# A gated mix of softmax and linear attention: the listed order made anew with longer landings of SyncE's transfers, and 120 packs on VectorE for 121

## The chip, the cores and the metric

The kernel runs on one core of a Trainium2 chip. The metric is the device time of one execution in microseconds (us); lower is better. A core has five engines that work side by side, each with a queue of its own that it runs strictly in order: TensorE (PE, matrix products), VectorE (DVE), ScalarE (ACT, here the exponential), GpSimd (POOL) and SyncE (SP, here the issue of transfers). They wait for one another by semaphores. A transfer (DMA) that SyncE issues lands some time later, and only then may an instruction that needs its data start.

## What is computed

The input x has 2048 tokens of 512 features, in bf16. Two branches with 32 heads of 16 features each work on it, and a gate per token mixes them:

```
x = A_x
g = _sigmoid((x * gate_w).sum(-1, keepdims=True))
a = _A_ref(x, A_wqkv, A_wo)            # softmax attention over all 2048 tokens, then @ wo
b = _B_ref(x, B_wqkv, B_w_phi, B_wo)   # linear attention
return g * a + (1 - g) * b

# _A_ref, per head:
scores = jnp.einsum("bhqd,bhkd->bhqk", q, k) * (Dh ** -0.5)
p = _softmax(scores, axis=-1)
o = jnp.einsum("bhqk,bhkd->bhqd", p, v)

# _B_ref, per head:
phi_q = jnp.concatenate([_softmax(pq, axis=-1), _softmax(-pq, axis=-1)], axis=-1)   # pq = q @ w_phi
phi_k = ...                                                                          # the same of k
kv = jnp.einsum("bhsf,bhsd->bhfd", phi_k, v);  z = phi_k summed over the tokens
o = (phi_q @ kv) / (phi_q . z + 1e-6)
```

Branch A is nearly all of the work: 32 heads times 2048 x 2048 exponentials.

## The kernel before

**Units and packs.** The queries are cut into 4 chunks of 512 (`QCH`), the keys into 16 tiles of 128. One unit is one head's scores for one tile of keys and one chunk of queries: a PSUM bank of 128 keys x 512 queries. Four heads side by side (in the four row groups of PE) make a pack, so there are 4 x 8 x 16 = 512 packs (`NPACK`). The 16 packs of one group of four heads and one chunk add their products of values into one bank; then the group is normalised (`_norm_a`, `_norm`).

**Two ways to an exponential.** Most packs go to ScalarE: the units run through a ring of five PSUM banks, and one ACTIVATE takes three units, the next two, in turn (`_qk`, `_exp`, line 1020). The other packs go to VectorE, which builds an approximate exponential from bit patterns: per unit one TENSOR_SCALAR turns scores into an integer whose bits are a bf16 number (`_vector_bits`, tile va, line 912), and three additions of constants per pair of packs give three shifted copies whose sum is a better exponential (`_vector_terms`, tile vp, line 928). PE then sums over four terms for such a pack and over one for a pack of ScalarE's (`_values`, line 1086). `AWAY` says which packs go to VectorE: one number for each of the 32 groups, whose five low bits stand for the packs 1, 4, 7, 10 and 13 of the group. `_plan_vector` collects a group's chosen packs in pairs; an odd one out stays alone.

**Side work.** In the cover of the exponentials run the projections of later heads (`_proj_k`, `_proj_v`, `_proj_q`), the gate (`_gate`), and branch B: features of k and their sums (`_b_quad`, `_b_kv`), features of q (`_b_quad`, `_b_phit`), their product with the sums (`_b_num`) and the output product (`_b_out`, `_out`), whose result is added to branch A's in PSUM.

**SyncE's transfers.** SyncE issues: copies of each projected q from qs into qT, which spread heads over the partitions (`_proj_q`, line 677, eight transfers each time); the gate's copies into gh (line 756, sixteen); the copies of normalised outputs from T2 into turned (`_norm`, line 1126, sixteen each time) and their transpose into onTA; the transposes of phi into phiT (`_b_phit`) and of branch B's results nb into WT (`_b_num`), all transposes through `_turn` (line 1341); the loads, and the stores of the output (line 1450).

**What sets the order.** Nothing in the program is ordered at run time. A planner (`Plan.order`) simulates the five queues once, before the program is written, and each engine then runs its list as planned. Each operation has an estimated cost, a due time (`prio`, in packs) and a landing (`lat`): the time after its planned end at which users on another engine may start. The planner takes the operation that can start first, and among those that could start at about that time the one with the smallest due time:

```
r = d.end + (d.lat if d.eng != e or e == "SP" else 0.0 if e == "PE" else self.CHAIN)
...
if o.ready <= t0 + 0.02 + (self.NEAR if pe else 0.0):
    more = self.COST * (o.until - array.SWITCH - base - o.cost) if pe else 0.0
    key = (o.prio + more, seq[id(o)])
```

So an estimate changes no instruction and no wait of the program: a semaphore still holds each user until its data is there. It changes only the places in the lists. `SHIFT` is a table that moves the due time of tagged pieces of work, in packs: p is a pack's product with its values, b the bits, t the terms and x the product with the terms of a pack on VectorE, k, v and q projections, g a group's normalisation, and d, e, a, f, h, n, o, w and y pieces of branch B and of the output. Three PSUM banks outside the ring are shared by all side work.

Of the kernel before, what the change touches and what calls it, by code (L numbers as in the profile page):

```python
# [376 lines left out]
class _Kernel:  # L377
# [10 lines left out]
    TURN = 1.5  # L388
# [278 lines left out]
    def _proj_q(self, qc, cp):  # L667
        n = qc * 4 + cp
        due = 32 * n + self.QDUE
# [7 lines left out]
        parts = [lambda e, r=r: e.dma_start(self.qT[r:r + DH, s0 + r // DH % 2, :], tile[r:r + DH, :])  # L677
                 for r in range(0, P, DH)]
        self.dma("SP", f"q{n}", parts, cost=0.63 * len(parts), reads=[self.b_qs[n % 2]], writes=[self.b_qT[s0]],
                 prio=due, lat=1.6)  # L680
# [44 lines left out]
    def _gate(self):  # L725
# [22 lines left out]
        for r, sign in ((0, -1.0), (1, 1.0)):  # L748
# [5 lines left out]
               prio=self.GATE + 4)  # L754
# [3 lines left out]
        d = self.dma("SP", "gate", parts, cost=0.6 * len(parts), writes=[self.b_g], deps=[a], prio=self.GATE + 5, lat=1.6)  # L758
        for b in self.b_onTA[0] + self.b_onTA[1]:
# [7 lines left out]
           prio=26)  # L767


    AWAY = (15, 5, 27, 9, 19, 31, 28, 28, 26, 27, 23, 27, 22, 30, 31, 22, 15, 15, 23, 7, 31, 23, 23, 7, 27, 31, 11, 27, 15, 31, 23, 31)  # L770

    SHIFT = (
# [723 lines left out]
```

## Time and profile before

| | |
|---|---|
| median of 3 runs | 760.5 us (760.5 to 760.85) |
| the profiled execution | 759.62 us |
| its span, first to last instruction | 757.8 us |
| ScalarE busy | 740.5 us (98%), 646 instructions |
| VectorE busy | 728.9 us (96%), 1130 instructions |
| PE busy (matmuls) | 716.8 us (95%), 7199 instructions |
| PE clock granted | 1.00 throughout |
| SyncE: qT, turned (issue, median to landing) | 0.59 and 0.60 us, 1.8 us |
| transposes: phiT, WT, onTA (median to landing) | 3.3, 2.5, 2.4 us |

"Busy" is the share of the span in which an engine has an instruction under way. A row of a group reads: line, engine, operation, output and input tile with their shapes, count | busy us, mean ns of one | idle time of the engine just before those instructions, and what ended it. In the timeline a row is a run of instructions: start, duration, engine, line, operation, and in brackets the wait before the first of them. "Landing" is counted from the start of a transfer's issue. In the chain, which is followed back from the last instruction, each piece is released by the one before it.

### The profile page before, as it was taken

The page shows a single profiled execution, that of the slowest core. Times are in us where ns is not written, and L with a number is a line of the kernel's source. Part 1 is how long each engine was busy: PE and PEld are TensorE (multiplying, and loading weights), DVE is VectorE, ACT ScalarE, POOL GpSimd, SP SyncE. Part 2 cuts the span into 40 slices and gives each one's busy share as a digit, 9 for nine tenths or more (in the row PEclk, how much of TensorE's full clock was granted, in tenths as well). Part 3 has the DMA queues.
Part 4 walks back from the last instruction along what each step waited for, and adds up shares of the span by engine and source line. Part 5 has one row for each costly group of instructions (what it writes and reads, how often), then busy time and mean ns, then how long its engine had stood idle before and what let it go on. Part 6 is the DMA issues. An engine that isn't in the chain of part 4 may idle for free.

```text
span 757.8 us, 16834 instructions
## 1 busy us (share of the span) xinstructions
PE 716.8 (95%) x7199; PEld 229.7 (30%) x7266; DVE 728.9 (96%) x1130; ACT 740.5 (98%) x646; POOL 7.8 (1%) x17
## 2 busy tenths in 40 slices
PE   8999999999899999999998999999999999999997
PEld 3343333233232322232222322222322322322322
DVE  6999999999999999999999999999999999999997
ACT  5999999999999999999999999999999999999996
POOL 3000000000000000000000000000000000000000
PEclk9999999999999999999999999999999999999999
DMA  9401001000010010100122111410203201131110
GB/s 196 147 6 15 9 1 16 8 3 13 9 15 8 5 18 2 15 8 4 20 24 47 23 16 21 84 22 9 35 17 72 41 8 22 37 63 22 11 26 29
DMA packets 90027, 21.78 MB, mean 29 GB/s; under 512 B 82912, under 2 KB 89440, under 8 KB 89952
## 3 DMA queue, kind: packets, MB, share of 16 engines
q1 hardware_dynamic: 88224, 20.17, 14.2%
q8 instruction: 57, 0.93, 0.5%
q10 hardware_dynamic: 1728, 0.52, 0.3%
q14 instruction: 18, 0.15, 0.1%
HBM read 4.21 MB, written 2.10 MB: 8 GB/s over the span
## 4 chain that ended last, share of the span: by engine, by line
ACT 63%; DVE 17%; PE 17%; DMA 2%; issue 1%; DVEq 0%
ACT ET L1020 60%; DVE va L912 7%; PE ps L972 6%; PE ps L1086 5%; DVE vp L928 4%; ACT bq L1259 3%; PE ps L641 2%; DMA WT<-nb 1%; DVE nb L1371 1%; DVE T L1107 1%; DMA xT<-in_A_x_dram 1%; DVE btree L1248 1%; PE ps L714 1%; PE ps L1389 1%; PE ps L1093 1%
## 5 line engine op out<-in xcount | busy, mean ns | idle before, releaser
L1020 ACT ACTIVATE ET<-ps 128x1536 bf16<-128x1536 f32 x626 | 712.2, 1340 | 8.5 <-PE ps L972 7.3
L972 PE MATMUL ps<-qT,kT 32*128 32x512 bf16 x2048 | 315.1, 384 | 16.2 <-ACT ET L1020 9.6
L912 DVE TENSOR_SCALAR va<-ps 128x512 uint16<-128x512 f32 x484 | 315.2, 684 | 9.6 <-PE ps L972 7.8
L928 DVE TENSOR_SCALAR vp<-va 128x4096 uint16<-128x4096 uint16 (+1 forms) x204 | 221.9, 1099 | 2.0 <-PE ps L1086 1.5
L972 PEld LDWEIGHTS ps<-qT,kT 32*128 32x128 bf16 x2048 | 81.3, 91 | 266.5 <-ACT ET L1020 156.0
L1086 PE MATMUL ps<-ET,V 128*32 128x512 bf16 x1564 | 150.2, 386 | 0.3 <-DVE va L912 0.3
L1086 PE MATMUL ps<-vp,vc 128*32 128x512 bf16 x968 | 86.1, 384 | 0.5 <-DVE vp L928 0.4
L1086 PEld LDWEIGHTS ps<-ET,V 128*32 128x32 bf16 x1564 | 39.6, 94 | 66.3 <-issue 53.7
L641 PE MATMUL ps<-WB,xT 128*128 128x512 bf16 x171 | 50.2, 383 | 4.2 <-issue 2.2
L1093 PE MATMUL ps<-kT,zero 128*32 128x512 bf16 x604 | 53.0, 385 | 0.0
L1086 PE MATMUL ps<-va,V 128*32 128x512 bf16 x484 | 47.4, 385 | 0.0
L1086 PE MATMUL ps<-vp,V 128*32 128x512 bf16 x484 | 47.0, 383 | 0.0
L641 PE MATMUL ps<-xT,WA 128*128 128x512 bf16 (+1 forms) x107 | 31.3, 374 | 4.8 <-issue 2.4
L1086 PEld LDWEIGHTS ps<-vp,vc 128*32 128x32 bf16 x968 | 22.3, 95 | 34.7 <-issue 20.7
L1259 ACT ACTIVATE bq<-bq 128x2048 bf16<-128x2048 bf16 x16 | 31.6, 1992 | 0.0
L1107 DVE STREAM_TRANSPOSE T<-ps 128x512 f32<-128x512 f32 x32 | 22.7, 708 | 1.6 <-PE ps L1086 1.5
L1230 DVE CAST bq<-ps 128x512 bf16<-128x512 f32 x32 | 21.7, 684 | 0.3 <-PE ps L641 0.2
L714 PE MATMUL ps<-WA,xT 128*128 128x128 bf16 x256 | 20.4, 220 | 0.7 <-DVE V L720 0.3
L1093 PEld LDWEIGHTS ps<-kT,zero 128*32 128x32 bf16 x604 | 13.7, 94 | 21.7 <-issue 19.6
L641 PEld LDWEIGHTS ps<-WB,xT 128*128 128x128 bf16 x192 | 12.6, 97 | 24.4 <-issue 12.9
L1257 DVE TENSOR_TENSOR bq<-bq,btree 128x2048 bf16<-128x2048 bf16 x16 | 19.5, 1219 | 0.0
L1389 PE MATMUL ps<-WoB,WT 128*128 128x512 bf16 x58 | 16.8, 382 | 2.6 <-DMA WT<-nb 1.1
(83 smaller groups left out, 338.0 us busy)
## 6 DMA issues: line engine op xcount, KB each, us to landing
turned<-T SPq DMA_DIRECT2D x240, 8.0 KB, 1.8
qT<-qs SPq DMA_DIRECT2D x120, 16.0 KB, 1.8
WB<-in_B_wqkv_dram SPq DMA_DIRECT2D x1, 1536.0 KB, 7.6
out_dram<-WB SPq DMA_DIRECT2D x12, 128.0 KB, 1.9
WA<-in_A_wqkv_dram SPq DMA_DIRECT2D x3, 384.0 KB, 5.9
WoA<-in_A_wo_dram SPq DMA_DIRECT2D x1, 512.0 KB, 7.7
WoB<-in_B_wo_dram SPq DMA_DIRECT2D x1, 512.0 KB, 8.6
WA<-in_A_wqkv_dram ACTq DMA_DIRECT2D x3, 128.0 KB, 4.2
```

Source lines behind the costliest of these rows:

```text
L641: ins = e.matmul(self._bank(job)[:, 0:n], lhs(c), rhs(c), start=(c == 0), stop=(c == 3))
L714: ins = e.matmul(self._bank(job)[:, P * tt:P * tt + P], self.xT[:, c, QCH * j + TOK * tt:QCH * j + TOK * tt + TOK], self.WA[:, 2, c, P * c ...
L912: parts.append(op("DVE", lambda e, j=j, job=job: e.tensor_scalar(self.va[:, pair, side, j, :], self._bank(job), SCALE * LOG2E * 128.0, (12 ...
L928: self.plan.op("DVE", lambda e, k=k, shift=shift: e.tensor_scalar(flat(self.vp[:, k]), flat(self.va[:, pair]), float(shift), None, op0=ALU ...
L972: return e.matmul(out, self.kT[32 * i:32 * i + 32, cp, kt * TOK:(kt + 1) * TOK], self.qT[32 * i:32 * i + 32, s, :], start=True, stop=True, ...
L1020: o = plan.op("ACT", lambda e: e.activation(self.ET[:, a % NS:a % NS + n, :], self.ps[:, self._ring(a):self._ring(a) + n, :], ACT.Exp, sca ...
L1086: ins = e.matmul(self._bank(ot)[32 * i:32 * i + 32, :], V[:, v0:v0 + 32], tile(), start=(kt == 0), stop=(kt == self.NT - 1), tile_position ...
L1093: ins = e.matmul(self._bank(ot)[32 * i:32 * i + 32, :], self.zero[:], self.kT[:, 0, 0:QCH], start=False, stop=False, tile_position=(0, 32 ...
L1107: op("DVE", lambda e: e.transpose(T1[:, side].rearrange("p b s -> p (b s)"), src()), 0.635, deps=last, writes=[b_T1[side]], name="n_t1", p ...
L1230: [lambda e, b, k=k: e.tensor_copy(bq[:, k].rearrange("p (g s v) -> p g s v", g=8, s=2)[:, :, 0, :], b.rearrange("p (g v) -> p g v", g=8))],
L1259: op("ACT", lambda e, side=side: e.activation(sides[side], sides[side], ACT.Exp, scale=1.0 - 2 * side), self.c_act(2048) + 0.04, reads=[bu ...
L1389: return e.matmul(self._bank(job), self.onTB[:, pr, tt * TOK:tt * TOK + TOK], self.WoB[:, pr, :], start=(pr == 0), stop=False)
```

## The change

Five estimates of landings after transfers on SyncE are longer, the table of packs on VectorE is another, with 120 packs where there were 121, and the table of shifts is another: of 708 entries 45 keep key and value, 161 keys are gone and 155 keys are new. No line that builds an instruction is changed.

```diff
-    TURN = 1.5
+    TURN = 2.2
...
         self.dma("SP", f"q{n}", parts, cost=0.63 * len(parts), reads=[self.b_qs[n % 2]], writes=[self.b_qT[s0]],
-                 prio=due, lat=1.6)
+                 prio=due, lat=2.6)
...
-        d = self.dma("SP", "gate", parts, cost=0.6 * len(parts), writes=[self.b_g], deps=[a], prio=self.GATE + 5, lat=1.6)
+        d = self.dma("SP", "gate", parts, cost=0.6 * len(parts), writes=[self.b_g], deps=[a], prio=self.GATE + 5, lat=4.0)
...
-    AWAY = (15, 5, 27, 9, 19, 31, 28, 28, 26, 27, 23, 27, 22, 30, 31, 22, 15, 15, 23, 7, 31, 23, 23, 7, 27, 31, 11, 27, 15, 31, 23, 31)
+    AWAY = (15, 5, 27, 26, 20, 27, 14, 28, 30, 13, 23, 31, 14, 14, 30, 31, 29, 14, 23, 7, 31, 27, 23, 23, 30, 31, 11, 27, 11, 31, 23, 31)
...
     SHIFT = (
-        ("p12", 2), ("k5", -3), ("k4", -9.5), ("v1", -6.5), ("p30", -8), ("p13", -1), ("p22", 1), ("q1", 3), ("w0",
-        -14), ("p18", -8.5), ("b1", -7.5), ("v2", -5), ("x1", -4), ("v4", 6), ("p21", -3), ("p2", 0.5), ("k1", -5),
...
+        ("k5", -3), ("k4", -10), ("v1", -6.5), ("p30", -4.5), ("p13", 7), ("p22", 8.5), ("q1", 3.5), ("w0", -10),
+        ("p18", -11.5), ("b1", -7.5), ("v2", -5), ("x1", -5), ("v4", 6), ("p21", -3), ("p2", 0.5), ("k1", -6),
...
             self.dma("SP", f"on{due:.0f}", parts, cost=0.68 * len(parts), reads=[b_T2], writes=[self.b_turned], prio=due,
-                     lat=1.6)
+                     lat=2.2)
...
         self.b_phiT.writers.append(self._turn(
             f"ph{t}", self.phiT[:, :, t % 4 * TOK:t % 4 * TOK + TOK], self.bq[:, k, :], self.b_bq[0:2],
-            self.phit_war, due, lat=2.2))
+            self.phit_war, due, lat=3.2))
```

`TURN` is the landing of every transpose for which `_turn` is given none: those of nb into WT and of turned into onTA. The transposes that load x have landings of their own, which stay.

185 rows, old and new, of the table SHIFT are left out of this document.

## The prediction

> **What bounds the kernel now.** I read the page's busy shares first, then the groups by shape for ScalarE, the waits of ScalarE and VectorE, the chain of waits, and last the timeline around the two longest gaps of ScalarE inside the run.
>
> From the page, the busy shares:
>
> ```profile
> span 757.8 us, 16834 instructions
> PE 716.8 (95%) x7199; PEld 229.7 (30%) x7266; DVE 728.9 (96%) x1130; ACT 740.5 (98%) x646; POOL 7.8 (1%) x17
> ```
>
> ScalarE (ACT) is idle for 17.3 us in all, VectorE (DVE) for 28.9. Both are nearly full, and ScalarE is the fuller. The groups of ScalarE by shape (busy us, mean ns | idle us before them), and then what ScalarE waited for (us in total, times, longest):
>
> ```profile
> L1020 ACT ACTIVATE ET<-ps 128x1536 bf16<-128x1536 f32 x313 | 485.6, 1551 | 7.7 <-PE ps L972 6.6
> L1020 ACT ACTIVATE ET<-ps 128x1024 bf16<-128x1024 f32 x312 | 352.3, 1129 | 0.7 <-PE ps L972 0.7
> L1020 ACT ACTIVATE ET<-ps 128x512 bf16<-128x512 f32 x1 | 0.8, 758 | 0.0
> ```
>
> ```profile
> ACT ET L1020 <- PE ps L972: 7.3, 6, 5.1
> ACT xT L1445 <- PE ps L1435: 3.7, 1, 3.7
> ```
>
> The exponentials take three score units, then two, in turn. Of the 7.3 us that they wait, 5.1 is the start (the first one begins at 8.71 us). That leaves five waits, 2.2 us, in all the time from 8.71 to the end of the last exponential at 750.20. Start and tail (750.20 to 757.8, 7.6 us, one head's normalisation, the last output product and its store) are set by loads and by a chain that the change does not shorten.
>
> The pace of ScalarE when nothing disturbs it, and what led to the two longest gaps, is in the chain of waits:
>
> ```profile
> 99.64 76.89 ACT ET L1020 x68
> 429.50 3.52 DMA WT<-nb
> 547.72 3.95 DMA WT<-nb
> ```
>
> 68 exponentials are 34 pairs of a three and a two: 76.89/34 = 2.26 us a pair. The transposes of nb into WT on SyncE landed 3.52 and 3.95 us after their issue, and the timeline shows ScalarE stopped soon after each:
>
> ```profile
> 433.12 0.48 DVE L1371 SCALAR_TENSOR_TENSOR nb<-ps,ghb,rb 128x256 bf16<-128x256 f32 x1 [0.73 <-DMA WT<-nb]
> 434.33 1.45 ACT L1020 ACTIVATE ET<-ps 128x1536 bf16<-128x1536 f32 x1 [0.51 <-PE ps L972]
> 551.81 1.02 PE L1389 MATMUL ps<-WoB,WT 128*128 128x512 bf16 x4 [1.09 <-DMA WT<-nb]
> 554.49 1.02 ACT L1020 ACTIVATE ET<-ps 128x1024 bf16<-128x1024 f32 x1 [0.72 <-PE ps L972]
> ```
>
> **All that an order can win.** 312 pairs at 2.26 us are 705.6; the last three adds 1.34 to the start of the single one, which takes 0.76 to its end; the 16 long exponentials of branch B cost 1.80 each (two take 3.60 in the chain), 28.8; the gate's one about 0.1. Together 736.6. From 8.71 to 750.20 are 741.5 us, so 4.9 us are lost inside: the 2.2 of the five waits, some 0.2 at each of them because an exponential no longer overlaps the next one, and small delays. Whatever the order, only these 4.9 us can come back.
>
> **The change, part by part.**
>
> One pack fewer on VectorE. The bits of the table of packs sum to 121 before and 120 after, so ScalarE has 4 x 392 = 1568 units for 1564: 314 threes and 313 twos, and no single. Where the single one began, now a two begins and a three ends the row. The two takes 2.26 - 1.34 = 0.92 to the next start, the three 1.55 to its end, against 0.76 before: 0.92 + 1.55 - 0.76 = 1.7 us more. This lies on the path whole: ScalarE's row between start and tail has only the 4.9 us of holes, and the tail begins at its end. VectorE loses four TENSOR_SCALAR of the bits (0.60 us apart in the chain, 2.4 us); there are 68 pairs of packs before and after, but 16 instead of 15 hold a single pack, so three term additions shrink from 1.17 to 0.69 us, 1.4 us. So 3.8 us less on VectorE, which is busy 702.5 of the 720 us from 20 to 740; it is not the row that ends the run, so I count it at nothing. The PE trades twelve tile matmuls of the three terms for four, two rows of four at 0.22 us, 0.4 us less, hidden beside ScalarE.
>
> The longer landings, place by place. They change no transfer, only when the planner expects a transfer's users to be ready, and so where it lists them.
> - Copies of q (1.6 to 2.6 us after the last issue; eight issues of 0.59 us, landing 1.8 median, 3.5 at most): the first score that needs a q stands 22 packs behind its projection by the due times, about 30 us at 724/512 us a pack, so both landings are hidden. Zero; if that cover were gone, 1.0 us a copy.
> - The gate's copies (1.6 to 4.0): issued from 38.9 to 48.6, landed 1.8 later, and the first transpose into onTA, which must follow them, is issued at 73.8. Zero.
> - Copies into turned (1.6 to 2.2) and their transpose into onTA (1.5 to 2.2): the only waiter seen is SyncE's own queue (10.4 us in 8 waits). Behind such a wait stand the next issues of SyncE: transposes of phi and nb, q, stores. It issues 120 q copies at 0.59, 240 turned at 0.60 and 47 transposes at about 1.25, some 274 us of 757.8, so it has room. Zero, with at most 0.6 us for each transpose queued there.
> - Transposes into phiT (2.2 to 3.2): planned at 1.31 + 2.2 = 3.5 us from issue, measured 3.3 median and 4.9 at most; no matmul that reads phiT shows a wait for a DMA. No gain; listed 1.0 us later its four users are covered by fills and values.
> - Transposes of nb (1.5 to 2.2): planned before at 1.25 + 1.5 = 2.75 us from issue, now at 3.45; measured 2.5 median. The two late ones missed the plan by 0.77 and 1.20 and stopped ScalarE for 0.51 and 0.72. With 0.70 us more room 0.7/0.77 of the one and 0.7/1.20 of the other would go: 0.46 + 0.42 = 0.9 us. Next late there is VectorE's own backlog: beside 553.64 it is in two term additions of 2.36 us.
>
> On the landing the Trainium skill (DMA: Bandwidth & Descriptors, "Anatomy of one DMA") has a rule that speaks against the change: a fixed 2.0 us and the bytes over 436 thousand per us, fitted on GpSimd's path. By it a 128 KB transpose lands in an estimated 2.3 us, the plan before covers every one, nothing comes back, and the sum is +1.7. The trace differs (2.4 to 3.9), and by its rows the sum of these two parts is 1.7 - 0.9 = +0.8.
>
> The new order. Of 708 shifts 45 keep key and value; the packs on VectorE differ in 15 out and 14 in. Which waits the new order has, the trace cannot show. Lower bound: none but landings, so the other 4.9 - 1.2 = 3.7 us go. Upper bound: the whole loss comes a second time, +4.9. I take the loss as it was, 4.9 in all: the two late landings are chances of this order (the median of the sixteen is 2.5 us), three of the five waits, 0.95 us, had nothing to do with SyncE, and the nearest row for another order over the same engines is this one. So the 0.9 is not credited.
>
> **Sum.** 757.8 + 1.7 = 759.5 us of span. The profiled execution took 759.62 with 1.8 outside its span, so 761.3; the median of the runs shown, 760.5, lies 0.9 above it, so 762.2 us, +0.22%. About 0.2%, 1.5 us, is what a measurement of this kernel can tell from no change, so this stands just on the slower side.
>
> **Rivals.**
> - No change that can be told: the 0.9 us of nb come back and no new wait takes their place: 760.5 + 0.8 = 761.3. For it: both long gaps do follow a landing. Against: a different order meets other late landings.
> - Faster: VectorE's 3.8 us of room pay on ScalarE. PE's weight loads for scores waited 35.7 us in 100 times for a bank that the bits on VectorE free, and those scores stand in PE's queue ahead of ScalarE's. If VectorE is never behind, the loss falls from 4.9 to about 1.3 (the waits not due to late banks or landings): 760.5 + 1.7 - 3.6 = 758.6. It decides where the loss is 1.7 us or less. For it: stretches of 77 and 51 us run without any loss. Against: two thirds of all the holes must go, over half of which are shorter than the page shows.
> - Slower by much more: a transpose of nb is queued on SyncE behind the eight issues of a q (5.00 us at 550.59), or behind a copy that waits for VectorE (up to 28.1 us for one). PE's queue is in order, so the output product and the scores behind it wait; one such case is 5.0 us less some 1.3 of an exponential under way, 3.7: 762.2 + 3.7 = 765.9. For it: one product already stopped PE for 1.09 us here. Against: the planner knows SyncE's queue and its costs (0.63 for 0.59).
> - The change does less than it says: the planner may place most users where they stood. Then only the pack is left, 762.2 again.
>
> **How the numbers follow.** Loss as before, or the change doing little: 0.41. Much slower: 0.12. Together slower 0.53. Same: 0.31. Faster: 0.16. The predicted time is 762.2. The ends are 762.2 - 4.9 = 757.3 and 762.2 + 4.9 = 767.1; leaving out about a tenth on each side I cut to 758.7 (the faster case) and 766.2 (the much slower one, a little over). The slower cases alone reach from 762.1 to 766.2.
>
> **What would show it.** 627 exponentials, 314 of 1536 columns and 313 of 1024, 480 bits, 204 term additions. The first exponential near 8.7 us, 7.6 us from the last one's end to the end. Five or so waits of ScalarE with 2 us in all: right. If they sum to under 0.5 us and ScalarE's row from first to last exponential is below 740 us, the faster rival holds. If SyncE's landings no longer stand ahead of a gap and nothing else does, the second. A single gap of ScalarE over 2 us with a DMA ahead of it shows the much slower one. The prediction would be wrong at its root if the spacing of the exponentials changed from 2.26 us a pair, or if the tail or start moved by over 1 us.

## The result, and the profile after

The changed kernel takes 757.51 us (median of 6 runs, 757.35 to 758.27), the kernel before 760.5 (759.91 to 762.88 beside it). The ratio is 0.9959 with a 95% interval of 0.9945 to 0.9972: 0.4% faster. The prediction was 762.2, 0.2% slower, with a range from 758.7: it missed in sign and in range. Run again later the changed kernel took 757.66, a ratio of 0.9957 (0.9942 to 0.9973).

The page of the changed kernel, its busy shares and the chain by engine:

```profile
span 755.7 us, 17044 instructions
PE 719.6 (95%) x7307; PEld 232.0 (31%) x7368; DVE 723.2 (96%) x1126; ACT 740.9 (98%) x647; POOL 7.8 (1%) x17
...
ACT 93%; PE 5%; DVE 1%; DMA 1%; issue 0%; DVEq 0%
```

In the chain of before ScalarE had 63%, VectorE and PE 17% each; now it is ScalarE almost alone. The groups of ScalarE by shape, and what ScalarE waited for (us in total, times, longest):

```profile
L1019 ACT ACTIVATE ET<-ps 128x1536 bf16<-128x1536 f32 x314 | 500.0, 1592 | 5.6 <-PE ps L971 5.3
L1019 ACT ACTIVATE ET<-ps 128x1024 bf16<-128x1024 f32 x313 | 367.2, 1173 | 0.0
...
ACT ET L1019 <- PE ps L971: 5.3, 2, 5.0
ACT xT L1444 <- PE ps L1434: 4.1, 1, 4.1
```

The counts are those forecast, 314 and 313. Of the five waits of before inside the row (0.28, 0.51, 0.72, 0.22 and 0.45 us) only the first is left, 0.28 at 13.5 us. The chain of waits now has stretches of the exponentials that run from one feature block of branch B to the next without a break:

```profile
235.18 80.45 ACT ET L1019 x71
...
368.91 91.76 ACT ET L1019 x81
...
567.71 84.54 ACT ET L1019 x75
```

**Where the time went.** The first exponential starts at 8.62 us (8.71 before) and the last ends at 747.69 (750.20), so the row took 739.07 us for 741.49, though it holds one pack more. By the prediction's pace (76.89/34 = 2.2615 us a pair) the work is 313 x 2.2615 + 1.55 + 28.8 + 0.1 = 738.3, so the loss inside fell from 4.9 to 0.8 us. The tail grew from 7.6 to 8.05. Together, span against span: 1.7 more work - 4.1 loss + 0.4 tail - 0.1 start = -2.1 us. The other 0.9 us between the medians is that the profiled execution of before (759.62) was one of its better ones: over all batches with it the kernel before ran from 758.9 to 765.7 with medians from 760.5 to 761.2, while the changed one stayed within 757.3 to 758.3. Two executions of the kernel before, of 1164.49 and 3253.5 us, stand outside this and are left out everywhere.

**Who waited for a transfer.** These are all waits for transfers among the engines' waits, first of the kernel before, then of the changed one:

```profile
POOL bq L574 <- DMA wphi<-in_B_w_phi_dram: 12.2, 1, 12.2
PEld ps L641 <- DMA xT<-in_A_x_dram: 1.4, 1, 1.4
PE ps L1389 <- DMA WT<-nb: 1.1, 1, 1.1
PE ps L641 <- DMA xT<-in_A_x_dram: 0.9, 1, 0.9
DVE nb L1371 <- DMA WT<-nb: 0.7, 1, 0.7
PEld ps L691 <- DMA xT<-in_A_x_dram: 0.4, 1, 0.4
```

```profile
POOL bq L574 <- DMA wphi<-in_B_w_phi_dram: 11.8, 1, 11.8
PEld ps L641 <- DMA xT<-in_A_x_dram: 1.1, 1, 1.1
POOL bq L728 <- DMA gw<-in_gate_w_dram: 0.6, 1, 0.6
PEld ps L691 <- DMA xT<-in_A_x_dram: 0.3, 1, 0.3
PE ps L641 <- DMA xT<-in_A_x_dram: 0.2, 1, 0.2
```

Only the loads at the start are left. To see the third case, which the waits put down to another engine, I laid the planner's own list beside the trace: each operation's planned start, shifted by as much as the exponentials around it ran behind plan, tells when its engine stood ready. In the kernel before three landings came after their first user stood ready: nb of token tile 1 by 0.75 us, nb of tile 7 by 1.20, and the transpose of turned into onTA of the last pair of groups but one by 0.64. Right behind them the spacing of the exponentials was 0.79, 1.04 and 0.76 us longer than usual, 2.6 us in sum. The visible idle time there is only 0.51, 0.72 and 0.45, because an exponential that is not held up overlaps the one before it. The third case in the trace of before:

```profile
728.82 1.27 SPq L1341 DMA_TRANSPOSE onTA<-turned  x1
...
731.69 0.38 PE L1389 MATMUL ps<-WoB,WT 128*128 128x512 bf16 x1 [0.86 <-DVE T L1107]
...
732.44 1.45 ACT L1020 ACTIVATE ET<-ps 128x1536 bf16<-128x1536 f32 x1 [0.45 <-PE ps L972]
```

The transpose landed at 731.23, and the instruction on VectorE that the trace names ended at 731.29; the product on PE depends on the transpose and not on that instruction.

In the changed kernel no landing after the loads overtook a user on an engine; the closest came some 0.6 us ahead. Two things did this, and the longer estimates are only one of them. The transposes of nb that stopped the kernel before are not slow in the new order: nb of tile 1 landed 3.2 to 4.0 us after its issue in each of the six profiles with the order of before, and 2.4 in each of the five with the new order, where its user also has 5 us of room. There nb of tile 3 is the slow one (3.5 to 3.7 us, 2.5 before), with 21 us of room. Had every user in the changed kernel stood earlier by what the estimates differ (0.7 us behind a transpose of nb or turned, 1.0 behind one of phi or the copies of a q, 2.4 behind the gate's), only the gate's copies, near the start, and those of three q would have come late there, by 1.4 us and by at most 0.4 us.

### The profile page after: what moved, and what is told of

It is laid out like the page before. It is cut to its first block, busy times and chain, and to the rows that moved or that the text cites. A ratio compares the mean times of both kernels' runs of the same rounds, so it can differ in the third digit from the quotient of the medians.

```text
span 755.7 us, 17044 instructions
## 1 busy us (share of the span) xinstructions
PE 719.6 (95%) x7307; PEld 232.0 (31%) x7368; DVE 723.2 (96%) x1126; ACT 740.9 (98%) x647; POOL 7.8 (1%) x17
## 4 chain that ended last, share of the span: by engine, by line
ACT 93%; PE 5%; DVE 1%; DMA 1%; issue 0%; DVEq 0%
ACT ET L1019 89%; ACT bq L1258 4%; PE ps L971 1%; PE ps L1085 1%; DMA xT<-in_A_x_dram 1%; PE ps L714 1%; PE ps L1388 0%; PE ps L1434 0%; PE ps L641 0%; DVE va L911 0%; PE ps L992 0%; DVE kT L664 0%; DVE qT L697 0%; ACT xT L1444 0%; DVE V L720 0%
## 5 line engine op out<-in xcount | busy, mean ns | idle before, releaser
L911 DVE TENSOR_SCALAR va<-ps 128x512 uint16<-128x512 f32 x480 | 311.5, 680 | 12.0 <-PE ps L971 9.5
L927 DVE TENSOR_SCALAR vp<-va 128x4096 uint16<-128x4096 uint16 (+1 forms) x204 | 219.2, 1086 | 0.9 <-PE ps L1085 0.6
L1092 PE MATMUL ps<-kT,zero 128*32 128x512 bf16 x744 | 63.3, 384 | 0.0
L641 PE MATMUL ps<-xT,WA 128*128 128x512 bf16 (+1 forms) x114 | 33.2, 375 | 2.8 <-issue 1.6
L1092 PEld LDWEIGHTS ps<-kT,zero 128*32 128x32 bf16 x744 | 16.0, 94 | 25.1 <-issue 22.2
L714 PEld LDWEIGHTS ps<-WA,xT 128*128 128x128 bf16 x256 | 15.1, 98 | 10.4 <-issue 6.9
```

What stands on the lines that cost most here:

```text
L641: ins = e.matmul(self._bank(job)[:, 0:n], lhs(c), rhs(c), start=(c == 0), stop=(c == 3))
L714: ins = e.matmul(self._bank(job)[:, P * tt:P * tt + P], self.xT[:, c, QCH * j + TOK * tt:QCH * j + TOK * tt + TOK], self.WA[:, 2, c, P * c ...
L911: parts.append(op("DVE", lambda e, j=j, job=job: e.tensor_scalar(self.va[:, pair, side, j, :], self._bank(job), SCALE * LOG2E * 128.0, (12 ...
L927: self.plan.op("DVE", lambda e, k=k, shift=shift: e.tensor_scalar(flat(self.vp[:, k]), flat(self.va[:, pair]), float(shift), None, op0=ALU ...
L1092: ins = e.matmul(self._bank(ot)[32 * i:32 * i + 32, :], self.zero[:], self.kT[:, 0, 0:QCH], start=False, stop=False, tile_position=(0, 32 ...
```

## Experiments

Three theories stand against each other. Late landings: the gain is that no landing overtakes its user. VectorE's room: the gain is the pack fewer. Denser tables: the new shifts would be better whatever the landings are. Where a run removes a wait, it does so by letting the transfer read x and write unused room, so the products of branch B and of some heads come out of stale data there; the amount of work, the lists and the sizes stay.

### Three late transposes that nobody waits for

```diff
+    ASIDE = ('dma_nb1', 'dma_nb7', 'dma_at481')
...
+        for o in p.queues["SP"]:
+            if o.name in self.ASIDE:
+                out, src = free.pop().rearrange("p (t q) -> p t q", t=4), self.xT[:, 3, D:2 * D]
+                o.fn = lambda e, out=out, src=src: e.dma_start_transpose(out, src)
+                aside.append(o)
+        for q in p.queues.values():
+            for o in q:
+                o.deps = [d for d in o.deps if d not in aside]
```

> The kernel before, its lists unchanged. Three transposes on SyncE (nb of token tile 1 and 7 into WT, turned into onTA of the last pair of groups but one) keep their places and sizes but read x and write unused room, and nobody waits for them; the products that used them read what stood there. Theory of late landings: in the trace of before these three landed 0.75, 1.20 and 0.64 us after the time at which their first user stood ready in its list, 2.6 us in sum, and ScalarE lost 0.79, 1.04 and 0.76 us right behind them; so about 2.6 us faster, span near 755.2, and no wait of ScalarE of over 0.3 us between its first and last exponential. Theory of VectorE's room: nothing on VectorE has changed, so within 0.4 us of before. Theory that the new tables are simply denser: also within 0.4 us.

The names are those of nb of tile 1 and 7 and of the transpose into onTA; `free` holds unused room.

Measured: 758.59 us (757.28 to 759.28), ratio 0.9955 (0.9938 to 0.9971), by the medians 2.6 us below before, the size forecast by late landings. The three holes were gone from the profile, but it had a new one: the span is 757.4 and not 755.2, and ScalarE waited 1.07 us at 462.34. PE had stood for a q:

```profile
458.70 0.59 SPq L694 DMA_DIRECT2D qT<-qs  x1
...
460.82 0.39 PE L989 MATMUL ps<-qT,kT 32*128 32x512 bf16 x1 [1.07 <-DMA qT<-qs]
...
461.25 0.69 DVE L929 TENSOR_SCALAR va<-ps 128x512 uint16<-128x512 f32 x1 [1.34 <-PE ps L989]
...
462.34 1.45 ACT L1037 ACTIVATE ET<-ps 128x1536 bf16<-128x1536 f32 x1 [1.07 <-PE ps L989]
```

The last copy of the eleventh q was issued at 458.70, 2.1 us behind the list's plan, and landed 2.1 us later. Its first user is a score for VectorE's bits, which the list has only 0.37 us behind the planned landing. So the kernel before has a fourth weak place, which its own profiled execution did not show: there this q landed 0.35 us in time. Places that give way in one execution and not in the next would make its runs scatter; the run without all four waits, below, bears this out.

### A control: three other transposes

> The same edit on three other transposes of the same kinds (nb of token tile 2 and 3, turned into onTA one pair of groups earlier), which landed before their users stood ready. Every theory: no change, within 0.4 us of before, and the waits of ScalarE at about 433.8, 553.8 and 732 us are still there.

Measured: 759.8 (759.02 to 761.78), ratio 0.9984 (0.9970 to 0.9998). That is 1.2 us below before by the ratio, outside the 0.4 us expected. So the control is not clean: about a third of the gain of the run above (3.4 us by its ratio) may come with the edit itself, or with landings of these three transposes that are late in some executions; this was not tried further. One of the three, nb of tile 2, came only 0.13 us ahead of its user in the profile of before. By the medians the run above is still 1.2 us below the control. The holes behind nb 1 and turned into onTA were there (0.74 and 1.20 us in the spacing) and one behind the q (0.78). The one behind nb 7 was not: in this run that transpose landed in time. So the expectation of three fixed places was too simple; the places are weak, and which of them give way changes from run to run.

### Less work on VectorE

```diff
+        m = n - 100 * (self.pairs > 12)
...
-                flat(self.vp[:, k]), flat(self.va[:, pair]), float(shift), None, op0=ALU.add),
+                flat(self.vp[:, k])[:, 0:m], flat(self.va[:, pair])[:, 0:m], float(shift), None, op0=ALU.add),
```

The run leaves out the last 100 columns of the term additions.

> The kernel before, its lists unchanged. From the 13th pair of packs on, the term additions on VectorE leave out their last 100 columns: 168 instructions shorter by some 23 ns, 3.9 us less work on VectorE, as much as one pack fewer takes off. Theory of VectorE's room: 2 to 4 us faster, ScalarE's loss down to about 1.5. Theory of late landings: under 0.6 us faster, because the three large holes of ScalarE wait for transfers and not for VectorE. Theory of denser tables: under 0.6 us.

Measured: 762.25 (759.15 to 764.10), ratio 1.0003 (0.9985 to 1.0021): no gain, and a gain of 2 us lies outside the interval. VectorE had its room (term additions of 217.0 us for 221.9, busy 726.4 for 728.9), and ScalarE's loss in the profiled execution was larger, 6.9 us: all four weak places gave way, by 1.27, 1.06, 1.19 and 1.30 us. Room on VectorE does not help against a landing.

### More work on VectorE in the changed kernel, first dose

> The changed kernel, its lists unchanged, with 68 very short writes added on VectorE, one ahead of every third term addition: at some 0.06 us each about 4 us more on VectorE, as much as one pack more. Theory of VectorE's room: 2 to 4 us slower than the changed kernel, so near before's time (759.5 to 761). Theory of late landings: up to 1 us slower than the changed kernel (757.5 to 758.5), and no wait of ScalarE over 0.5 us.

Measured: 757.88 (757.37 to 758.36), ratio 0.9951 (0.9934 to 0.9969). This tells nothing on VectorE's room, because the dose failed: the 68 short writes began and ended while the instruction ahead of them still ran, and busy VectorE rose by 0.6 us only.

### The same with a true dose

```diff
+                if k == 0:
+                    e.tensor_scalar(self.more[:, self.mores:self.mores + 1], self.iden[:, 0:1], 1.0, None, op0=ALU.add)
+                    self.mores += 1
```

> The run with short writes on VectorE again with a true dose: there the 68 writes began and ended within the instruction ahead of them and cost VectorE nothing (busy 723.8 for 723.2). Now each of the 68 reads a column and adds a constant, at an estimated 0.06 to 0.1 us each 4 to 7 us more on VectorE, one pack's worth or more. Theory of VectorE's room: 2 to 5 us slower than the changed kernel (759.5 to 762.5). Theory of late landings: within 1 us of it (757 to 758.5), no hole of ScalarE over 0.5 us between 14 us and its last exponential.

Measured: 758.26 (757.87 to 758.92), ratio 0.9962 (0.9950 to 0.9974), about 0.7 us above the changed kernel, which ran in another batch. The 68 instructions now push the next one back by 63 ns each (median), 4.3 us in sum, a pack's worth. ScalarE still has no wait but the start and one of 0.3 us. With the run of less work, VectorE's room is refuted in both directions, as the cause of a gain of this size.

### Four waits away, and then a pack

The q of the first experiment was taken out in the same way.

> As the run without the three waits, and the copies of the eleventh q into qT go the same way (they read x, write unused room, nobody waits): in that run they landed 1.59 us after the first score that needs them stood ready, at 459 us, and ScalarE lost 1.39 us there. Theory of late landings: span near 755.2, no wait of ScalarE over 0.3 us between 14 us and its last exponential, 3 to 4.5 us faster than before by the medians, and runs that scatter by no more than the changed kernel's (0.9 us). Rival, that a hole shut in one place opens in another: within 0.5 us of the run without the three waits, with a new hole elsewhere.

Measured: 757.90 (757.45 to 758.24), ratio 0.9957 (0.9942 to 0.9972), by the medians 2.9 us below before, just under the 3 to 4.5 forecast. The span of the profiled run, 756.1, is 0.9 above the forecast, 0.3 of it a later start (first exponential at 9.03 us) and 0.25 the tail. All holes of the four places are gone, with no new one, and the scatter is 0.8 us in 5 runs, for 3.5 in 17 of before:

```profile
L1040 ACT ACTIVATE ET<-ps 128x1536 bf16<-128x1536 f32 x313 | 487.0, 1556 | 7.0 <-PE ps L992 5.9
L1040 ACT ACTIVATE ET<-ps 128x1024 bf16<-128x1024 f32 x312 | 354.0, 1135 | 0.0
```

So the old list with 121 packs, cured of its late landings alone, gains 2.9 us, and the whole change gains 3.0. The row lost 2.6 us instead of 4.9. That the two gains agree is partly chance: the change also pays for a pack and finds a denser list, and these two nearly cancel, as the next run and the account of the prediction show.

```diff
-    AWAY = (15, 5, 27, ..., 27, 15, 31, 23, 31)
+    AWAY = (15, 5, 27, ..., 27, 7, 31, 23, 31)
```

> The same with one pack fewer on VectorE (number 28 of the table of packs, its fourth bit: the lists differ only from about 650 us on). By the price of a pack on ScalarE's row: 1.2 to 1.8 us slower than the run without the four waits, span 756.4 to 757.0. Theory of VectorE's room: the 3.9 us less on VectorE shut as much on ScalarE, so within 0.5 us of it.

Measured: 759.12 (758.69 to 759.57), ratio 0.9978 (0.9968 to 0.9987), 1.2 us above the run without the four waits. The row grew by 1.2 us (739.21 to 740.38): 1.7 of work, 0.5 less loss. A pack fewer on VectorE is a cost, somewhat below the 1.7 us worked out. Whether the 0.5 us comes from VectorE's room or from the other order behind 650 us was not tried.

### Transposes made late in the changed kernel

```diff
+    LATER = ('dma_nb2', 'dma_nb7', 'dma_at481')
...
+            if o.name in self.LATER:
+                extra = [lambda e, out=room.pop(): e.dma_start_transpose(out, self.xT[:, 3, D:2 * D])
+                         for _ in range(2)]
+                o.fn = extra + [o.fn]
```

> The changed kernel, its lists unchanged, with three transposes made late: ahead of nb of token tile 2 and 7 and of turned into onTA of the last pair of groups but one, SyncE issues two more transposes of the same size (of x, into unused room), 2.5 us of issue, and the users wait for all. They had landed 1.23, 1.09 and 0.91 us before their users stood ready, so they come 1.3, 1.4 and 1.6 us too late. Theory of late landings: ScalarE loses that about one for one behind each, 3 to 4.5 us slower than the changed kernel (760.5 to 762), with holes near 460, 556 and 731 us. Theory of VectorE's room or of denser tables: within 0.6 us of the changed kernel.

Measured: 764.62 (763.33 to 766.74), ratio 1.0050 (1.0031 to 1.0068), 7 us above the changed kernel: the mechanism as forecast, the size above the range. What ScalarE waited for, and the place of the largest wait:

```profile
ACT ET L1032 <- PE ps L984: 11.8, 6, 5.0
...
736.29 1.44 PE L1401 MATMUL ps<-WoB,WT 128*128 128x512 bf16 x3 [2.31 <-DMA onTA<-turned]
...
738.32 1.45 ACT L1032 ACTIVATE ET<-ps 128x1536 bf16<-128x1536 f32 x1 [3.00 <-PE ps L984]
...
742.16 6.88 ACT L1032 ACTIVATE ET<-ps 128x1536 bf16<-128x1536 f32 x6 [1.31 <-PE ps L984]
```

Behind the two nb the spacing of the exponentials was 1.23 and 1.53 us longer for some 1.4 and 1.55 us of lateness: one for one. Behind the transpose into onTA it was 4.6 us for about 2.1. There PE stood for 2.31 us, and from about 735 to 742 us the clock granted to it, 1.00 until then, was halved. Stretches of the trace show it: from and to, length, busy time of PE, PEld, DVE, ACT and POOL with counts, the granted clock, the DMA share and GB/s.

```profile
728.00:735.00 7.00, 5.53 (x56) 1.79 (x54) 6.74 (x11) 7.00 (x7) 0.00 (x0) 1.00 0.40 79
735.00:742.00 7.00, 5.71 (x19) 1.17 (x19) 2.84 (x4) 2.79 (x3) 0.00 (x0) 0.51 0.07 16
742.00:750.00 8.00, 7.76 (x95) 2.33 (x91) 7.38 (x13) 7.84 (x7) 0.00 (x0) 1.00 0.01 2
```

At the halved clock the three matmuls of the output product took 1.44 us, where three of the same shape take 0.82 at 1.00 (at 732.46 us in the first run above), the scores behind them were slower too, and ScalarE ran dry a second time. The forecast of one for one has no such term. How the 4.6 us divide between the stop and the clock was not tried apart. What lowers the clock is not shown either: it fell within this stop, while the stops of 1.46 and 1.73 us behind the two nb came with no lower clock.

The scatter is back too (3.4 us), and a lower clock goes with the slow end of it. Of the 26 runs of the kernel before beside the first experiments, the eight slowest, from 762.17 us up, were all granted 0.998 or less on average (0.993 in the slowest), and of the other 18 all but one 0.999 or more.

### Each part of the change alone

> The kernel before with the five longer landings alone: its table of packs (121) and its shifts stay. If longer landings by themselves are the cure, the late landings go and nothing else: near 757.9, as in the run without the four waits. If the shifts only fit the landings that they were made for, the planner's list itself comes out loose: it has ScalarE stand for 6.2, 2.3, 2.1 and 1.1 us at four places, and the last exponential 16 us later than in the list before, with side work left over behind it, so 30 to 40 us slower than before (790 to 800). No landing comes after its user stood ready in either case.

> The changed kernel with the five landings of before: its tables (120 packs, the new shifts) stay. If the new tables are a better list whatever the landings are, near 757.5 to 760. If they only fit their landings, the list has ScalarE stand for 10.7, 9.5, 5.5, 5.0, 3.1 and 2.2 us at six places, and the run takes 800 to 810 us.

Measured, one run each: 805.0 us for the landings alone and 816.47 for the tables alone, somewhat beyond the expected 790 to 800 and 800 to 810. The planner's times are those at the full clock, and the granted one was 0.974 and 0.988 on average (0.50 from 775 to 792 us in the first, in the work left over at the end). In the first that work is what shows most, in the second ScalarE's holes:

```profile
ACT xT L1445 <- PE ps L1435: 27.7, 1, 27.7
ACT ET L1020 <- PE ps L972: 21.9, 19, 6.1
```

```profile
ACT ET L1019 <- PE ps L971: 30.2, 15, 9.4
ACT bq L1258 <- DVE bq L1256: 19.4, 3, 10.8
```

None of the parts is good alone: the shifts were made for one set of landings, and under another the list falls apart. So the new tables are not better whatever the landings are, and these two runs do not sum to the change. They do bear on the landings: laid beside its list as above, the first has no landing that overtook its user (the closest came 0.5 us ahead, as expected), and in the second nb of tile 1 landed 4.3 us after its issue and 1.6 us late, with the granted clock at 0.57 from 454 to 462 us behind it. That fits longer estimates as what keeps landings ahead of their users, but the two lists differ in everything else as well.

### The longer landings with 121 packs

The groups 28 to 30 of the table of packs hold one pack more, and 195 shifts in the later part differ, chosen by the planner's own end.

> The five longer landings with 121 packs: the changed kernel with one pack more on VectorE (the groups 28 to 30 of the table of packs changed), and shifts made anew for the last part of the list, with the planner's end as the only measure. In that list the last exponential comes 0.8 us earlier than in the changed kernel's and the end 0.8 us later. If the gain of the change lies in the landings and not in the pack: no landing overtakes a user, runs scatter by about 1 us, and the time is 0.3 to 1.3 us above the changed kernel run beside it, well below before (757.8 to 759). If the 120 packs carry the gain: near before, 760 or more.

> The changed kernel once more, beside the run with 121 packs on the same chip. Every theory: 757.3 to 758.3.

Measured: 758.83 (758.21 to 760.06), ratio 0.9971 (0.9960 to 0.9983) with 121 packs; 757.66 (757.33 to 758.27) for the changed kernel beside it. With 121 packs 1.9 us of the changed kernel's 3.0 us are there, so the gain is not the pack's. Two things were not as expected: the runs scatter by 1.9 us and not 1, with the two slowest at a granted clock of 0.997, and one landing overtook its user, a transpose of phi by 0.3 us, with no hole behind it; the transpose into onTA that is the third weak place of before came only 0.04 us ahead. The row of ScalarE is 0.6 us shorter than the changed kernel's (738.46 for 739.06) and the tail 1.5 longer (9.56 for 8.05), as in the list. No version here beats the changed kernel.

## Why the prediction was wrong

- That ScalarE bounds the kernel, and that only its loss inside the row can come back, held: the loss went from 4.9 to 0.8 us, and start and tail moved by 0.1 and 0.4.
- The pack was priced at 1.7 us and counted on the path. The row holds 1.7 us more work in the changed kernel, and the run with the waits away lost 1.2 us by it. VectorE's 3.8 us were counted at nothing, which both doses nearly bear out (no gain for less work, 0.7 us for 4.3 more).
- **The step that failed is the one on the new order: "I take the loss as it was, 4.9 in all", with the 0.9 us of the nb transposes not credited.** The late landings were worth 2.3 us of the profiled row (741.49 to 739.21 without them) and 2.9 of the median. They were not "chances of this order": the list before places users 0.1 to 0.4 us behind planned landings that are too short, and in each of the four profiles that keep all or some of these waits at least one of the four places gave way, in the profiles of the changed kernel none. The median of the sixteen transposes, 2.5 us, hid that nb of tile 1 is slow in every profile of this order. The argument by the nearest row, that another order over the same engines loses as much, is what should have been doubted, since the change lengthens just the estimates that this order breaks on.
- Three terms beneath it were mis-sized. The holes were read from visible idle time (1.23 us for the two nb) where the spacing lost 1.83. The copies of q were set to zero because the first score stands 22 packs behind: that holds for ScalarE's scores, but scores for VectorE's bits are listed far ahead, and the eleventh q had 0.37 us of room, which failed in three of the four profiles here that wait for it. And the transpose into onTA was set to zero because only SyncE's queue was seen to wait, while the trace put PE's wait at 731.69 down to VectorE; it was the third hole, 0.76 us, and one of the three waits said to have nothing to do with SyncE. It landed a normal 2.42 us after its issue. It was late because SyncE issued it 1.1 us behind the plan; in the changed kernel it is issued 1.2 us behind plan and still lands 1.1 us ahead of its user.
- The remaining gain lies in the list itself. Between the run with 120 packs and four waits away and the changed kernel the row shrank from 740.38 to 739.07, 1.3 us. So the row goes from 741.49 by 2.3 us less for the landings, 1.2 more for the pack and 1.3 less for the list to 739.07. The planner's own list for before has 2.98 us of gaps between exponentials, for the changed kernel 1.55, 1.4 us less. That the new shifts are a better find there is read from the lists and rows and was not tried apart. The planner itself has the changed kernel no faster: in its list the last exponential ends 0.3 us later than before and the end comes 0.8 us later, so by its own times there was nothing to gain, and what the runs gained is what the kernel before loses beyond its plan.
- The median of before was taken as the profiled time plus a constant 0.9. It is no constant: it vanished with the late landings (757.54 profiled for a median of 757.51 in the changed kernel, 757.90 for 757.90 with the four waits away).
- Of the rivals, the faster one had its sign and nearly its place (758.6 for 757.5) by a wrong mechanism; the one with the nb transposes had the right mechanism and credited a third of it. The much slower one, a transpose stuck on SyncE, occurred only where it was made.
- The Trainium skill's rule (DMA: Bandwidth & Descriptors, "Anatomy of one DMA — SWDGE (gpsimd) path"), a fixed 2.0 us and the bytes over 436 thousand per us, was fitted on GpSimd's path and puts these transposes at an estimated 2.3 us. No run here is on that path, and on SyncE it is no bound: transposes of 128 KB from nb landed between 2.4 and 4.5 us after their issue in these runs, and it is the late ones that cost. Why one lands at 2.4 and another at 4 us stays open. It is not mere chance, since nb of tile 1 is slow in every profile of one order and of tile 3 in every one of the other.

## What to carry to other kernels

Where the order of work is fixed ahead of time, an estimate of a transfer's landing should cover the late landings and late issues, not the median: a user listed too early stops an in-order engine and all behind it, and the stop can cost more than it lasts when the clock falls behind it. Before judging a list, count for each transfer how much room its first user has and compare it with the spread of landings of that same transfer over several runs; in this case the kernel whose runs scattered was the one that waited for transfers. Here tables tuned against one set of estimates were worth nothing under another, so such a change is to be judged as a whole.

## What was not expected of the hardware

- An instruction's duration is not its price. In the changed kernel the exponentials' mean durations are 1592 and 1173 ns against 1551 and 1129 before, and the median spacing from one to the next is the same (1.33 and 0.90 us). The unbroken row is not the reason, since with the true dose the row has no more breaks and the means are 1558 and 1138 ns; what is stays open.
- A write of one constant column on VectorE (59 ns) cost its queue nothing, a short instruction that reads a column 63 ns of 149.
- The landing of a transfer scatters enough to set a kernel's scatter: the kernel before ran from 758.9 to 762.4 us, and in the same batch, with four waits out of the way, from 757.45 to 758.24.
- A late landing can cost twice its lateness: one of about 2.1 us made PE stand for 2.31 us and came with some 7 us at half the granted clock, and ScalarE lost 4.6 us behind it.
